# The last 512 tokens of a first pass as one chunk, keys put in order in halves, and another written order of the work, in a kernel of windowed attention and two MLPs

## The chip, the core and the metric

The kernel runs on one core of a Trainium2 chip. The metric is device time in microseconds (us) for one execution; three runs of the kernel before are shown. TensorE (PE) multiplies and transposes and writes only PSUM; its weight loads (PEld) run beside its matmuls. VectorE (DVE), ScalarE (ACT) and GpSimd (POOL) do the element work, and SyncE (SP) issues all transfers between the memory of the chip and SBUF. Each engine works through its own list of instructions in the order in which they were written, and waits on semaphores for what it needs from the others.

## What is computed

Attention with 8 heads on two sequences of 768 tokens: each query sees the 31 keys nearest to it and 24 block maxima of the keys, with the block means of the values behind them. Then come two MLPs with 512 inputs, 2048 hidden units and 512 outputs on the 1536 tokens. The second has a rational function of its hidden values.

```python
k_sum = k.reshape(B, H, nb, block, D).max(axis=3)      # block 32, window 16
v_sum = v.reshape(B, H, nb, block, D).mean(axis=3)
mask_l = np.abs(pos[:, None] - pos[None, :]) < window
...
scores_all = np.concatenate([scores_l_m, scores_s], axis=-1)
a = np.exp(scores_all - max); a = a / (sum + 1e-09)
out = np.matmul(a, np.concatenate([v, v_sum], axis=2))
...
h = np.maximum(x @ w_in, 0.0);  x = h * h @ w_out       # first MLP
h = x @ w_in2;  g = P(h) / (Q(h) + 1e-6);  out = g @ w_out2
```

## The kernel before

**Four passes.** The MLP work stands in `steps`: pass 0 covers hidden blocks 0 to 4 of the first MLP, pass 1 blocks 5 to 15, passes 2 and 3 the second MLP. A step is one token chunk with one block of 128 hidden units. It has a first layer (`l1`, line 567, four parts of three matmuls into a tile h), element work (`elem_1` to `elem_5`: relu on ScalarE, the square on VectorE, a rounded copy sh on ScalarE, the rest sl on GpSimd), and a second layer (`l2`, line 661, four parts of three matmuls into tiles y). Every product is made of three matmuls because each operand is split into a rounded part and a rest (wh and wl, xh and xl, sh and sl). In pass 0 a chunk has 256 tokens (`tok1`, six chunks, 30 steps); in the later passes it has 512 (`tok2`, three chunks). With 256 tokens the sums y need two PSUM banks, with 512 four.

**The attention fills pass 0.** It is cut into 24 units d = 0 to 23; four units give the 512 features of one group of 256 tokens, so chunk c of pass 0 needs the units 4c to 4c+3. A unit goes through: q (transpose of the queries, PE), z (copy into qz, ScalarE), s (scores pss, PE), m (mask and minimum, VectorE, line 467), e (exponential, ScalarE, line 476), r (sum and reciprocal rs, VectorE, lines 484 and 485), n (scaling of pr, GpSimd, line 491), p (transpose into ptp, PE), b (copy pp, ScalarE or VectorE, line 505), o (product with the values, pav, PE), x (xh, ScalarE) and y (xl, VectorE, line 536). The keys of a head pair come by E (transfer), P (put in order, GpSimd, line 300), t (transposes pk, PE), l and k (copies into kt), c and B (block maxima).

**Weights** arrive as 512 KB pieces: I (transfer into one of three buffers), T (ScalarE, line 150), D (VectorE, lines 158 and 159), W (wh, ScalarE) and M (wl, GpSimd, line 175).

**What sets the order.** All of the attention and nearly all of pass 0 is written by hand in the string `ORDER`; every word is one of the letters above with its number (h, i, j, G, H and Y are l1, elem_1, elem_2, elem_4, elem_5 and l2; a star puts a copy on VectorE). Each engine gets its instructions in this order. After the list, `main_loop` runs from step 28 (G1). While attention lasts, the sums of pass 0 hold two PSUM banks (`O0`), and the tiles of the attention take turns in the other four.

Of the kernel before, what the change touches and what calls it, by code (L numbers as in the profile page):

```python
# [9 lines left out]
F32 = mybir.dt.float32  # L10
# [49 lines left out]
def tile_window_attention_moe_moe(  # L60
# [13 lines left out]
    nc = tc.nc  # L74
    B, H, S, D = q.shape
    NT, DM = out.shape
    DFF = w_in1.shape[1]
    P = 128
# [3 lines left out]
    NP = H // 2  # L82
    KC = DM // P
    NF = DFF // P
    LO = 64
# [116 lines left out]
    ]  # L202
    kst = const.tile([P, TR, 4, D], F32, tag="xh2", name="kst")[0:VP]
    vst = const.tile([P, 4, TR, D], F32, tag="xl2", name="vst")[0:VP]
    ksrc = {}
    vsrc = {}
    banks = ["y0", "y1", "y2", "y3", "a0", "a1"]

# [649 lines left out]
```

## Time and profile before

| | us |
|---|---|
| median of three runs | 616.33 (616.15 to 616.97) |
| the profiled execution, its own time | 617.99 |
| its span | 616.3 |
| TensorE busy in the span | 597.6 (97%) |
| VectorE, ScalarE, GpSimd busy | 390.8, 402.1, 345.9 |
| granted TensorE clock, mean | 0.999 |

The span is what the trace shows between first and last instruction; 1.7 us of the profiled execution lie around it. Times within the trace count from the span's start. A matmul's recorded time holds its run through the array as well, so neighbours overlap in the record; the distance between starts is what one costs in a row of them.

### The profile page before, as it was taken

The page shows a single profiled execution, that of the slowest core. Times are in us where ns is not written, and L with a number is a line of the kernel's source. Part 1 is how long each engine was busy: PE and PEld are TensorE (multiplying, and loading weights), DVE is VectorE, ACT ScalarE, POOL GpSimd, SP SyncE. Part 2 cuts the span into 40 slices and gives each one's busy share as a digit, 9 for nine tenths or more (in the row PEclk, how much of TensorE's full clock was granted, in tenths as well). Part 3 has the DMA queues.
Part 4 walks back from the last instruction along what each step waited for, and adds up shares of the span by engine and source line. Part 5 has one row for each costly group of instructions (what it writes and reads, how often), then busy time and mean ns, then how long its engine had stood idle before and what let it go on. Part 6 is the DMA issues. An engine that isn't in the chain of part 4 may idle for free.

```text
span 616.3 us, 9787 instructions
## 1 busy us (share of the span) xinstructions
PE 597.6 (97%) x3488; PEld 514.0 (83%) x3488; DVE 390.8 (63%) x815; ACT 402.1 (65%) x766; POOL 345.9 (56%) x363
## 2 busy tenths in 40 slices
PE   5899998999999999999999999999999999999997
PEld 4789898999988888888888888888888888888885
DVE  5998777666553332111256487898878887686775
ACT  5887566766554443222356598988888887777772
POOL 4777858355664445222557568675656664454442
PEclk9999999999999999999999999999999999999999
DMA  9999894440342331000045202121202200010011
GB/s 220 247 225 213 208 233 96 120 108 16 114 160 72 99 103 35 0 1 0 1 137 179 96 1 69 34 70 34 69 35 69 69 1 0 1 69 1 22 47 68
DMA packets 64145, 51.48 MB, mean 84 GB/s; under 512 B 39777, under 2 KB 56161, under 8 KB 64097
## 3 DMA queue, kind: packets, MB, share of 16 engines
q1 hardware_dynamic: 64096, 50.87, 30.8%
q8 instruction: 27, 0.44, 0.3%
q14 instruction: 22, 0.17, 0.1%
HBM read 47.71 MB, written 3.15 MB: 83 GB/s over the span
## 4 chain that ended last, share of the span: by engine, by line
PE 80%; DVE 1%; ACT 0%; POOL 0%; issue 0%; DVEq 0%; ACTq 0%
PE h L567 39%; PE y L661 38%; PE pss L452 1%; PE pav L517 1%; PE ptp L501 1%; DVE acc L687 0%; PE pt L433 0%; DVE h L616 0%; DVE q L613 0%; ACT h L609 0%; POOL wl L175 0%; DVE p L619 0%; ACT q L588 0%; DVE p L602 0%; DVE pp L505 0%
## 5 line engine op out<-in xcount | busy, mean ns | idle before, releaser
L567 PE MATMUL h<-xh,wh 128*128 128x512 f32 (+1 forms) x444 | 161.9, 365 | 0.0
L567 PE MATMUL h<-xh,wl 128*128 128x512 f32 (+1 forms) x444 | 160.1, 361 | 0.0
L567 PE MATMUL h<-xl,wh 128*128 128x512 f32 (+1 forms) x444 | 160.0, 360 | 0.0
L637 POOL TENSOR_TENSOR sl<-r,sh 128x512 fp32r<-128x512 f32 (+1 forms) x63 | 66.4, 1054 | 119.8 <-PE y L661 76.6
L591 POOL TENSOR_TENSOR q<-q,u 128x512 f32<-128x512 f32 x48 | 63.8, 1330 | 94.7 <-ACT q L588 91.0
L582 DVE TENSOR_TENSOR r<-r,h 128x512 f32<-128x512 f32 (+1 forms) x63 | 35.0, 555 | 113.1 <-ACT r L577 105.6
L567 PEld LDWEIGHTS h<-xh,wh 128*128 128x128 f32 x444 | 83.8, 189 | 12.8
L567 PEld LDWEIGHTS h<-xh,wl 128*128 128x128 f32 x444 | 83.7, 189 | 12.9
L567 PEld LDWEIGHTS h<-xl,wh 128*128 128x128 f32 x444 | 83.8, 189 | 12.4
L175 POOL TENSOR_TENSOR wl<-wdec,wh 128x512 fp32r<-128x512 f32 x64 | 83.3, 1309 | 12.5 <-ACT wh L170 10.5
L661 PE MATMUL y<-sl,wh 128*128 128x512 f32 (+1 forms) x252 | 85.7, 340 | 1.3 <-POOL sl L637 1.3
L661 PE MATMUL y<-sh,wh 128*128 128x512 f32 (+1 forms) x252 | 86.7, 344 | 0.0
L661 PE MATMUL y<-sh,wl 128*128 128x512 f32 (+1 forms) x252 | 85.2, 338 | 0.0
L577 ACT ACTIVATE r<-h 128x512 f32<-128x512 f32 (+1 forms) x63 | 31.1, 494 | 82.5 <-PE h L567 44.1
L661 PE MATMUL y<-wh,sl 128*128 128x512 f32 x192 | 74.8, 390 | 0.1
L661 PE MATMUL y<-wl,sh 128*128 128x512 f32 x192 | 74.7, 389 | 0.0
L661 PE MATMUL y<-wh,sh 128*128 128x512 f32 x192 | 74.7, 389 | 0.0
L637 POOL TENSOR_TENSOR sl<-p,sh 128x512 fp32r<-128x512 f32 x48 | 64.5, 1344 | 9.9 <-ACT sh L630 8.6
L613 DVE SCALAR_TENSOR_TENSOR q<-q,h 128x512 f32<-128x512 f32 x48 | 32.9, 685 | 39.4 <-ACT h L609 39.4
L159 DVE SCALAR_TENSOR_TENSOR wdec<-wraw,wdec 128x512 int32<-128x512 int32 x64 | 56.0, 875 | 2.2
L170 ACT CAST wh<-wdec 128x512 fp32r<-128x512 f32 x64 | 39.7, 621 | 22.6 <-DVE wdec L159 22.5
L661 PEld LDWEIGHTS y<-sl,wh 128*128 128x128 f32 x252 | 47.6, 189 | 6.9 <-POOL sl L637 1.5
(88 smaller groups left out, 1071.8 us busy)
## 6 DMA issues: line engine op xcount, KB each, us to landing
wraw<-in_moe_w_in_dram SPq DMA_DIRECT2D x32, 512.0 KB, 3.9
wraw<-in_moe_w_out_dram SPq DMA_DIRECT2D x32, 512.0 KB, 3.4
early<-in_v_dram SPq DMA_DIRECT2D x40, 96.0 KB, 4.4
out_dram<-acc SPq DMA_DIRECT2D x12, 256.0 KB, 2.1
acc<-in_q_dram SPq DMA_DIRECT2D x10, 256.0 KB, 5.4
early<-in_k_dram SPq DMA_DIRECT2D x4, 384.0 KB, 5.3
early<-in_v_dram SPq DMA_DIRECT2D x4, 384.0 KB, 8.0
kst<-in_k_dram SPq DMA_DIRECT2D x8, 192.0 KB, 7.1
```

The costliest lines, as they stand in the source:

```text
L159: nc.vector.scalar_tensor_tensor(out=t, in0=low, scalar=29, in1=t, op0=ALU.logical_shift_right, op1=ALU.bitwise_or)
L170: nc.scalar.copy(out=wt[n][0][:, j], in_=f32(wdec[n, j]))
L175: nc.gpsimd.tensor_tensor(out=tl[:, j], in0=t, in1=f32(th[:, j]), op=ALU.subtract)
L452: nc.tensor.matmul(pt[:, c * HK:(c + 1) * HK], lhsT=qz[d % 2][:, c].rearrange("p e t -> p (e t)"), rhs=kt[p][:, 2 * i + c], start=c == 0, ...
L501: nc.tensor.transpose(out=pt[0:HK, c * P:(c + 1) * P], in_=pr[:, c, 0:HK], identity=ident)
L567: nc.tensor.matmul(hq[g][:, 0:n], lhsT=w[:, 0, ws], rhs=x[:, part, ts], start=(part == 0 and j == 0), stop=(part == KC - 1 and j == 2),)
L577: nc.scalar.activation(out=r, in_=hq[g][:, 0:n], func=AF.Relu)
L582: nc.vector.tensor_tensor(out=eq[g], in0=eq[g], in1=hq.pop(g)[:, 0:n], op=ALU.mult)
L591: nc.gpsimd.tensor_tensor(out=q_, in0=q_, in1=u_, op=ALU.mult)
L613: nc.vector.scalar_tensor_tensor(out=q_, in0=q_, scalar=1.0 + 1e-6, in1=z_, op0=ALU.add, op1=ALU.mult)
L637: nc.gpsimd.tensor_tensor(out=sl[:, 0:n], in0=eq.pop(g), in1=f32(sh[:, 0:n]), op=ALU.subtract)
L661: nc.tensor.matmul(o, lhsT=lt, rhs=rt, start=(f == 0 and j == 0 and d * m % 512 == 0), stop=(f == FS[ps] - 1 and j == 2 and (d + 1) * m % ...
```

## The change

`tok1` has five chunks: four of 256 tokens and one of 512, the last. Pass 0 has 25 steps instead of 30, and `main_loop` begins at step 23. The last chunk needs the units 16 to 23. Its `h` and `Y` words (h80 to h99, Y80 to Y99) stand for matmuls with 512 columns.

The keys of the first sequence are put in order in two halves, P and R, each with its own choice of engine; the transposes read the copy. P0 is on VectorE, the others on GpSimd. The tiles pp, mx and rs are named by the parity of d instead of being taken in turn, so the units may be written out of order. `ORDER` is another string.

```diff
-    def k_rel(p, copy):
+    def k_rel(p, b, copy):
         t = early[4 + p][0:VP].rearrange("p (r h d) -> p r h d", r=TR, d=D)
-        copy(out=t.rearrange("p r h d -> p h r d"), in_=ksrc[p])
-        ksrc[p] = t
+        rs = slice(b * TR // 2, (b + 1) * TR // 2)
+        copy(out=t[:, rs].rearrange("p r h d -> p h r d"), in_=ksrc[p][:, :, rs])
+        krel[p] = t
...
-        mx = ap.tile([P, 8], F32, tag="mx", name="mx", bufs=2)
+        mx = mxs[d % 2]
...
-    tok1 = [(G * c, G) for c in range(NT // G)]
+    tok1 = [(G * c, G) for c in range(NT // G - 2)] + [(NT - 2 * G, 2 * G)]
...
-        P=lambda p: k_rel(p, nc.gpsimd.tensor_copy), t=k_tr,
+        P=lambda p, c=nc.gpsimd.tensor_copy: k_rel(p, 0, c),
+        R=lambda p, c=nc.gpsimd.tensor_copy: k_rel(p, 1, c), t=k_tr,
...
-    "E0 E1 _id P0 _m0 t0 l0 P1 E2 q_0 _z0 t1 q0 k0 _pr k1 I0 P2 q_1 _ml t2 _m1 E3 q1 l1 z0 c0 T0 "
+    "E0 _id _m0 _ml P0* _bw R0 E1 q_0 t0 E2 l0 I0 P1 R1 t1 q0 k0 _m1 P2 q_1 R2 _z0 E3 q1 l1 c0 t2 "
```

At the start, GpSimd had in the kernel before (ident is the unit matrix, early the keys, mask and bw constants):

```order
masks.py:197 MEMSET ident 128x128
masks.py:199 ISA
masks.py:199 AFFINE_SELECT ident<-ident 128x128
L300 COPY early<-early 96x2x8x64 x3
L248 AFFINE_SELECT mask<-mask 64x96 x2
L300 COPY early<-early 96x2x8x64
L264 AFFINE_SELECT bw<-bw 96x24 x2
```

and has now, with what each row waits for:

```order
masks.py:197 MEMSET ident 128x128
masks.py:199 ISA
masks.py:199 AFFINE_SELECT ident<-ident 128x128 [waits Pool_49]
L265 AFFINE_SELECT bw<-bw 96x24 [waits DVE_49]
L265 AFFINE_SELECT bw<-bw 96x24 [waits Pool_49]
L302 COPY early<-early 96x2x4x64 [waits DMAHW0_49]
L302 COPY early<-early 96x2x4x64 [waits DMAHW1_49]
```

The selects on bw moved ahead of the key copies, and the first of them waits for VectorE. VectorE now begins with:

```order
L274 MEMSET mask 64x96
L275 MEMSET mask 128x6x24
L302 COPY early<-early 96x2x4x64 [waits DMAHW0_49]
L263 MEMSET bw 96x120
L270 MEMSET bw 96x96 [waits DVE_49]
L367 MEMSET pk 128x5x4 x4
```

Half of the first key copy moved here, and the bw and pk constants stand behind it; before, the first two pk constants were VectorE's second row.

At the end of the attention TensorE had (y_2188 is half of the sums of chunk 4; h there is chunk 4's as well):

```order
L567 MATMUL h<-xh,wh 128x256
L567 MATMUL h<-xl,wh 128x256
L567 MATMUL h<-xh,wl 128x256
L501 MATMUL ptp<-ident,pr_96 120x128 x4
L501 MATMUL ptp<-ident,pr_97 120x128 x4
L517 MATMUL pav<-pp,early 64x64 x32
L661 MATMUL y_2188<-sh,wh 128x256
```

and has now (the sums y are those of chunk 3, the 512-column rows are chunk 4's first):

```order
L519 MATMUL pav<-pp_87,early 64x64 x8
L519 MATMUL pav<-pp_88,early 64x64 x8
L503 MATMUL ptp<-ident,pr_103 120x128 x4
L569 MATMUL h<-xh,wh 128x512
L569 MATMUL h<-xl,wh 128x512
L569 MATMUL h<-xh,wl 128x512
L503 MATMUL ptp<-ident,pr_102 120x128 x4
L663 MATMUL y_1822<-sh,wh 128x256
L663 MATMUL y_1822<-sh,wl 128x256
L663 MATMUL y_1822<-sl,wh 128x256
L519 MATMUL pav<-pp_88,early 64x64 x8
L519 MATMUL pav<-pp_87,early 64x64 x8
```

The matmuls of chunk 4 moved from before and between the last units to behind them. ScalarE's list there now reads:

```order
L478 ACTIVATE pr_103<-pr_103,mx_90 128x120 x4
L478 ACTIVATE pr_102<-pr_102,mx_89 128x120 x4
L533 CAST xh<-pav 128x256
L507 COPY pp_87<-ptp 120x512
L507 COPY pp_88<-ptp 120x512
L533 CAST xh<-pav 128x256 x3
L147 ACTIVATE wdec<-wraw 128x512
L507 COPY pp_87<-ptp 120x512
L533 CAST xh<-pav 128x256 x2
```

where before it was:

```order
L476 ACTIVATE pr_96<-pr_96,mx 128x120 x4
L476 ACTIVATE pr_97<-pr_97,mx 128x120 x4
L577 ACTIVATE r<-h 128x256
L630 CAST sh<-r 128x256
L505 COPY pp<-ptp 120x512
L531 CAST xh<-pav 128x256
L170 CAST wh<-wdec 128x512
L531 CAST xh<-pav 128x256 x2
L170 CAST wh<-wdec 128x512
L531 CAST xh<-pav 128x256
```

Three of the last copies of pp are ScalarE's now, between exponentials and xh.

## Rows read from the trace of the kernel before

**Rows 1.** The page: busy time of TensorE, and its share of the span.

```profile
PE 597.6 (97%) x3488; PEld 514.0 (83%) x3488; DVE 390.8 (63%) x815; ACT 402.1 (65%) x766; POOL 345.9 (56%) x363
```

**Rows 2.** Busy time by stage (us); each engine's instructions; clock; DMA share; GB/s.

```profile
core 0: us, PE busy (x) PEld busy (x) DVE busy (x) ACT busy (x) POOL busy (x), PEclk, DMA share, GB/s
0.00:5.58 5.58, 0.00 (x1) 0.01 (x1) 1.72 (x14) 1.28 (x1) 1.80 (x9) 1.00 0.69 173
5.58:33.18 27.60, 23.41 (x200) 20.23 (x201) 23.71 (x92) 22.81 (x59) 18.54 (x33) 1.00 1.11 253
33.18:66.00 32.82, 31.66 (x321) 30.30 (x318) 29.55 (x102) 26.61 (x68) 25.07 (x36) 1.00 1.01 207
66.00:100.00 34.00, 31.45 (x311) 30.57 (x310) 24.71 (x73) 21.98 (x59) 23.53 (x35) 1.00 0.88 212
100.00:130.00 30.00, 28.93 (x311) 28.05 (x310) 19.61 (x75) 21.72 (x60) 18.45 (x37) 1.00 0.35 89
130.00:156.00 26.00, 25.67 (x286) 25.07 (x285) 17.10 (x63) 17.17 (x48) 11.93 (x26) 1.00 0.23 60
156.00:176.00 20.00, 20.00 (x147) 18.99 (x146) 11.68 (x17) 10.29 (x23) 11.49 (x12) 1.00 0.37 123
```

**Rows 3.** TensorE's waits between 66 and 156 us: us, times, longest.

```profile
PE y L661 <- POOL sl L637: 1.3, 1, 1.3
PE pav L517 <- ACT pp L505: 1.2, 1, 1.2
PE pav L517 <- DVE pp L505: 1.2, 2, 0.9
```

**Rows 4.** The chain that ended last, in order of time: start, us, what.

```profile
110.52 2.86 PE h L567 x24
...
182.33 2.72 PE h L567 x12
```

**Rows 5.** The start, in order of time: start, us, engine, line, operation [idle before].

```profile
4.49 1.03 POOL L300 COPY early<-early 96x1024 f32<-96x1024 f32 x1 [3.05 <-DMA early<-in_k_dram]
5.58 1.54 PE L368 MATMUL pk<-ident,early 96*128 96x96 f32 x8 [5.58 <-POOL early L300]
...
7.29 1.54 PE L368 MATMUL pk<-ident,early 96*128 96x96 f32 x8 [0.17 <-POOL early L300]
8.62 0.63 PE L433 MATMUL pt<-ident,acc 128*128 128x128 f32 x2
```

**Rows 6.** VectorE, 0 to 175 us, by form: count, busy us, mean ns.

```profile
L505 DVE COPY pp<-ptp 120x512 f32<-120x512 f32 x17 | 11.5, 684 | 5.4 <-PE ptp L501 3.0 <-PE pav L517 2.2 <-issue 0.2
L257 DVE COPY mask<-mask 128x384 f32<-128x384 f32 x1 | 0.4, 353 | 0.0
L262 DVE MEMSET bw<- 96x120 f32 x1 | 0.2, 158 | 0.0
```

**Rows 7.** ScalarE from 66 to 73 us, in order of time.

```profile
69.38 0.67 ACT L150 ACTIVATE wdec<-wraw 128x512 f32<-128x512 f32 x1 [1.49 <-DMA wraw<-in_moe_w_out_dram]
69.95 1.23 ACT L476 ACTIVATE pr<-pr,mx 128x120 f32<-128x120 f32 x4
71.09 0.56 ACT L505 COPY pp<-ptp 120x512 f32<-120x512 f32 x1
```

**Rows 8.** VectorE's second weight step alone, and the same beside other work.

```profile
152.99 0.69 DVE L159 SCALAR_TENSOR_TENSOR wdec<-wraw,wdec 128x512 int32<-128x512 int32 x1
...
32.47 1.64 DVE L159 SCALAR_TENSOR_TENSOR wdec<-wraw,wdec 128x512 int32<-128x512 int32 x1
```

**Rows 9.** The last units of the attention, all engines, in order of time.

```profile
145.66 2.40 ACT L476 ACTIVATE pr<-pr,mx 128x120 f32<-128x120 f32 x8
...
147.99 2.75 POOL L491 TENSOR_SCALAR pr<-pr,rs 128x120 f32<-128x120 f32 x8 [1.34 <-DVE rs L485]
...
151.19 1.15 PE L517 MATMUL pav<-pp,early 120*64 120x64 f32 x32
...
152.87 0.38 ACT L531 CAST xh<-pav 128x256 fp32r<-128x256 f32 x1
```

More of the change, by code (lines that the diff above doesn't have):

```diff
@@ L187, in tile_window_attention_moe_moe @@
     qz = [ap.tile([P, 4, 2, LO], F32, name=f"qz{j}", bufs=1) for j in range(2)]
+    pps = [ap.tile([HK, 4, 2, LO], F32, name=f"pp{j}", bufs=1) for j in range(2)]
+    mxs = [ap.tile([P, 8], F32, name=f"mx{j}", bufs=1) for j in range(2)]
+    rss = [ap.tile([P, 4], F32, name=f"rs{j}", bufs=1) for j in range(2)]
     kss = [ap.tile([P, NB], F32, name=f"kss{j}", bufs=1) for j in range(NP)]
@@ L205, in tile_window_attention_moe_moe @@
     ksrc = {}
+    krel = {}
     vsrc = {}
@@ L360, in k_tr @@
     def k_tr(p):
-        src = ksrc[p].rearrange("p r h d -> p r (h d)")
+        src = (krel if p < NP else ksrc)[p].rearrange("p r h d -> p r (h d)")
         pk[p] = [bank("pk"), bank("pk")]
@@ L482, in d_r @@
         mx, pr = ex.pop(d)
-        rs = ap.tile([P, 4], F32, tag="rs", name="rs", bufs=2)
+        rs = rss[d % 2]
         nc.vector.tensor_reduce(out=mx[:, 4:8], in_=pr, axis=AX.X, op=ALU.add)
@@ L503, in d_b @@
     def d_b(d, copy=nc.scalar.copy):
-        pp = ap.tile([HK, 4, 2, LO], F32, tag="pp", name="pp", bufs=2)
+        pp = pps[d % 2]
         copy(out=pp.rearrange("p c e t -> p (c e t)"), in_=po[d][0:HK])
```

67 rows, old and new, of the table ORDER are left out of this document.

## The prediction

> **What bounds the kernel now.** I read the page first: TensorE is busy for 597.6 us of the 616.3 us span [rows 1]. Then the stages [rows 2]: from 156 us on, TensorE is busy all the time, so nothing but fewer or shorter matmuls shortens that part. Ahead of it lie 156 us with 141.1 us of TensorE work (23.41 + 31.66 + 31.45 + 28.93 + 25.67). The 14.9 us that are missing split into 5.6 before the first transpose, 4.2 up to 33 us, 1.2 up to 66, 2.6 up to 100, 1.1 up to 130 and 0.3 up to 156. The reader is to see two more things there. Up to 33 us VectorE is busy for 23.71 of 27.60 us and the DMA share is 1.11, so TensorE waits for VectorE and for data, not for its own order. And from 130 to 156 us TensorE waits for only 0.3 us, because the matmuls of chunks 4 and 5 fill in between the last units of the attention. Third come TensorE's waits between 66 and 156 us [rows 3]: one wait of 1.3 for sl, one of 1.2 for a copy pp by ScalarE, and 1.2 for copies pp by VectorE. The sum below counts gains and losses in these places alone: the TensorE work itself, the start, the middle, and the end of the attention.
>
> **The longer last chunk.** Two chunks of 256 tokens are 10 steps with 24 matmuls, 240 of 256 columns; the one chunk is 5 steps, 120 matmuls of 512 columns. In a row, 24 of the narrow ones take 2.86 us, 0.119 each, and 12 of the wide ones 2.72, 0.227 each [rows 4]. So 240 x 0.1192 = 28.6 us become 120 x 0.2267 = 27.2 us: 1.4 us less TensorE work, all of it on the bounding engine. Element work gets longer per instruction and fewer in number; after the attention the three other engines are at half load (156 to 176 us [rows 2]), which hides it. Wide steps follow each other at 2.7 us per layer, while relu, square, sh and sl of one step need about 3.2 us in a row and have two wide layers (5.4 us) to hide in. If that cover fails, each of five steps could lose some tenths.
>
> [...]
>
> **The start.** Now TensorE starts at 5.58 us, when the copy of the first keys on GpSimd, 4.49 to 5.52, is done [rows 5]. In halves on two engines each half should take about half as long. The order shows what takes it back. The first half stands on VectorE, and behind it the bw and pk constants that the first transpose and GpSimd wait for. No row shows this half copy. Its bounds are 353 ns (a copy of 384 columns) and 684 ns (512 columns from PSUM) [rows 6]; I take 0.47, 353 x 512 / 384, since that row reads SBUF too. Then 4.49 + 0.47 + two constants of at most 0.16 each + the pk constant puts the first transposes at about 5.4 instead of 5.58. GpSimd waits with its selects on bw for the first of these constants (5.1), and only then copies the second half, half of 1.03 us: done at about 6.1. The second four transposes then run 6.1 to 6.8, and end about when the eight end now (5.58 + 8 x 0.166 = 6.9; a set of eight takes 8.62 - 7.29 = 1.33 [rows 5]). I take 0.1 gained, bounds 0.5 gained and 0.3 lost. Up to unit 7 the list holds the same VectorE work as before within 0.5 us (instructions counted, times their rows), and this stretch goes by VectorE and data, so I expect nothing else here, within 1 us either way.
>
> **The middle, 56 to 110 us.** The wait of 1.2 us for a pp by ScalarE [rows 3] has a clear cause [rows 7]: ScalarE stood 1.49 us for a weight piece that had not landed, then did an exponential of 1.23 us, then the copy. In the new list that piece stands behind 768 KB fewer transfers, some 3 us at the 212 to 253 GB/s of these stages [rows 2], and the copy is VectorE's, behind a weight step and a mask step. If the weight step is done early, nothing is waited for; if not, about 0.7 us. I take 0.4 instead of 1.2: 0.8 gained, bounds 1.2 and 0. For the other waits there (sl, 1.3, and pp, 1.2) I see no change of load: from the scores of unit 12 to the second layer of step 14 the list gives VectorE some 22.5 us against 20.7 of TensorE, before 20.3 against 18.3 (instructions counted, times their rows). Zero, bounds 2.4 gained and 2 lost.
>
> **The end of the attention.** Here the change takes something away. h80 reads all of the units 16 and 20, h83 those of 19 and 23, so no matmul of the last chunk can fill gaps before the last units are through. Before, 25.67 of 26.00 us were filled [rows 2]. What is left to fill with is chunk 3 only. Between h79 and h80 TensorE has four transposes p of 0.42, six products o of 0.62, two scores s of 0.85 and three parts of Y of 0.36, 8.2 us; ScalarE has 9.6 us in the same piece of list (three exponentials of 1.2 [rows 9], three copies pp of 0.6, six xh of 0.33, and a qz, a weight step, a relu and a sh with 2.2). The one place where I find TensorE early is the product of unit 20: its pp waits on ScalarE behind the exponentials of units 23 and 22 and one xh. Followed from unit 18's scores with the pitches of rows 9 (exponentials 1.2, n 1.38, pp 0.6, xh 0.33, o 0.6), with all engines free at the start, TensorE waits there for 0.9 us. Against the 0.3 of before that is 0.6 lost. If ScalarE comes in late by the 2.4 us of two exponentials in a row [rows 9], TensorE waits that much longer, 3.3. So the loss is 0.6, with bounds of 0 and 3.0.
>
> What could make it more is VectorE's weight step 18, which stands ahead of the xl of unit 21, on which h81 waits; it takes 0.69 us alone and took 1.64 beside other work [rows 8]. The longer one would delay h81 by about 1 us, for 615.6 in all; the sum goes by 0.69, and 1.64 is in the range. [...]
>
> **The sum.** -1.4 - 0.1 - 0.8 + 0.6 = -1.7. The profiled execution took 617.99 us with a span of 616.3; its changed twin should have a span of 614.6. The median of 616.33 happens to equal that span, and the change of -1.7 taken from it gives 614.6.
>
> **Rivals.** *The middle keeps its waits.* VectorE is the fuller engine there in both lists, and a wait removed at one product comes back at the next Y; the new list may also bring small waits of its own. Then -1.4 - 0.1 + 0.6 = -0.9 and some tenths more: 615.6. For it speaks that VectorE has more work than TensorE in that stretch; against it, that the late weight piece was the cause of one wait and stands earlier now. *The end starves TensorE.* If ScalarE and VectorE reach the last eight units late, the wait is 3.3 us or more instead of 0.9, and if the middle gains nothing: 616.33 - 1.5 + 3.0 + 0.4 = 618.2, slower. For it speaks that the products of units 16 to 23 now stand within 11 us of TensorE work, where 25 us were; against it, the walk above. It decides from 3.0 us of TensorE waiting between the scores of unit 18 and h83. *More is gained.* If the middle loses its waits of 1.2, 1.3 and 0.9: 616.33 - 1.5 - 3.0 + 0.6 = 612.4. *The halves do nothing* is in the forecast already, with 0.1.
>
> **How the numbers follow.** A measurement of this kernel can tell about 0.2%, 1.23 us, from no change: faster is below 615.1, slower above 617.6. Forecast 0.42, the middle keeps its waits 0.28, the starved end 0.20, more gained 0.10. Most of the forecast's case and all of the larger gain are faster, 0.50; the rest of it and the second case are the same, 0.29; the starved end is slower, 0.21. The range of 8 in 10 reaches from 612.6 to 617.7: it leaves out half of the larger gain and more than half of the starved end. The forecast's own range is 613.8 to 615.4.
>
> **What would show it.** In the profile after: wide matmuls of the last chunk at 0.227 us; the first transposes at 5.3 to 5.5 us in two groups of four with a gap between; no ScalarE wait for a weight piece near 68 us; TensorE busy without a gap from h83 on, and its waits in the 15 us ahead of it at 1 us in sum, at the product of unit 20. Wrong would be a wait of over 2 us there, new waits of over 2 us between 10 and 110 us, or a first chunk of pass 1 that starts late.

## The result and the profile after

The changed kernel takes 610.82 us (median of 6 runs, 610.05 to 613.01) against 616.38 us for the kernel before (median of 6, 615.80 to 619.22). The ratio is 0.9906 (95% interval 0.9882 to 0.9930); a second set of runs gave 0.9916 (0.9895 to 0.9937). By the two ratios it is faster by 5.8 and 5.2 us; below, 5.5 stands for it. The forecast was 1.7 us, and the range ended at 612.6: the sign was right, the size was not, and the time lies 1.8 us below the range.

The profiled execution took 610.05 us, its span is 608.3. First the page's line of busy times, which answers to [rows 1]:

```profile
PE 595.7 (98%) x3368; PEld 509.1 (84%) x3368; DVE 381.1 (63%) x803; ACT 402.6 (66%) x764; POOL 346.1 (57%) x361
```

TensorE is busy for 1.9 us less, in a span 8.0 us shorter (the profiled execution of the kernel before was 1.6 us over its median). So 6.1 us between these two executions are idle time of TensorE. Its place is in the busy time by stage, cut as in [rows 2] (columns as there):

```profile
5.58:33.18 27.60, 24.77 (x205) 22.66 (x206) 25.05 (x99) 23.65 (x64) 19.63 (x36) 1.00 1.17 250
33.18:66.00 32.82, 32.59 (x327) 31.44 (x326) 25.76 (x88) 26.46 (x70) 27.25 (x39) 1.00 1.02 226
66.00:100.00 34.00, 33.84 (x361) 33.04 (x360) 27.28 (x93) 27.32 (x73) 25.07 (x42) 1.00 0.94 204
100.00:130.00 30.00, 30.00 (x326) 29.39 (x326) 22.67 (x102) 24.63 (x72) 19.26 (x38) 1.00 0.38 95
```

Idle in these four: 2.83, 0.23, 0.16 and 0.00 us, where it was 4.19, 1.16, 2.55 and 1.07. A second profile of each kernel, taken with the experiments, confirms only the later part. Up to 33 us it has the idle time the other way round, 3.00 us in the kernel before (first line) and 4.29 in the kernel after:

```profile
5.58:33.18 27.60, 24.60 (x203) 21.40 (x203) 23.30 (x92) 23.58 (x62) 18.80 (x34) 1.00 1.10 254
5.58:33.18 27.60, 23.31 (x204) 21.47 (x205) 25.25 (x99) 23.38 (x64) 19.41 (x36) 1.00 1.16 247
```

From 33 to 156 us the second pair has 3.4 us of idle time before and 0.3 after, the first pair 5.1 and 0.4. So the change takes 3 to 5 us of idle time out of this part, and what it does ahead of 33 us is less than two executions differ by.

TensorE's waits, as in [rows 3] (us in total, times, longest), first from 5.7 to 66 us, then the one that is left from 66 to 156 us:

```profile
PE pk L370 <- DVE pk L367: 5.6, 1, 5.6
PE pk L370 <- POOL early L302: 1.1, 2, 0.8
PE pav L519 <- DMA early<-in_v_dram: 0.7, 2, 0.4
PE pss L454 <- DVE kt L396: 0.6, 1, 0.6
PE pvs L409 <- POOL early L327: 0.6, 1, 0.6
...
PE pss L454 <- DVE mx L469: 0.2, 1, 0.2
```

The 5.6 us are the time to the first transpose, which has not moved. The chain of work that ended last shows the long chunk, as in [rows 4] (start, us, what):

```profile
144.46 5.44 PE y L663 x24
```

5.44 / 24 is 0.2267 us for a matmul of 512 columns, as forecast. The start, as in [rows 5]:

```profile
4.57 0.42 DVE L302 COPY early<-early 96x512 f32<-96x512 f32 x1 [3.39 <-DMA early<-in_k_dram]
4.97 0.16 DVE L263 MEMSET bw<- 96x120 f32 x1
5.36 0.13 DVE L367 MEMSET pk<- 128x20 f32 x4
...
5.20 0.47 POOL L265 TENSOR_SCALAR_AFFINE_SELECT bw<-bw 96x24 f32<-96x24 f32 x2 [3.76 <-DVE bw L263]
5.61 1.72 POOL L302 COPY early<-early 96x512 f32<-96x512 f32 x3
...
5.58 2.88 PE L370 MATMUL pk<-ident,early 96*128 96x96 f32 x16 [5.58 <-DVE pk L367]
```

VectorE's half takes 0.42 us (0.47 was estimated), and the constants behind it bring the first transpose back to 5.58 us, as before.

### The profile page after: what moved, and what is told of

Its sections match the earlier page's. It is cut to its first block, busy times and chain, and to the rows that moved or that the text cites. A ratio compares the mean times of both kernels' runs of the same rounds, so it can differ in the third digit from the quotient of the medians.

```text
span 608.3 us, 9541 instructions
## 1 busy us (share of the span) xinstructions
PE 595.7 (98%) x3368; PEld 509.1 (84%) x3368; DVE 381.1 (63%) x803; ACT 402.6 (66%) x764; POOL 346.1 (57%) x361
## 4 chain that ended last, share of the span: by engine, by line
PE 90%; DMA 3%; SPq 3%; DVE 2%; ACT 1%; issue 1%; DVEq 0%; ACTq 0%
PE h L569 43%; PE y L663 41%; DMA early<-in_v_dram 3%; PE pss L454 3%; PE pav L519 2%; PE ptp L503 1%; SPq L136 1%; SPq L336 1%; PE pt L435 1%; DVE acc L689 0%; SPq L315 0%; SPq L355 0%; SPq L293 0%; DVE h L618 0%; DVE q L615 0%
## 5 line engine op out<-in xcount | busy, mean ns | idle before, releaser
L569 PE MATMUL h<-xl,wh 128*128 128x512 f32 (+1 forms) x424 | 156.6, 369 | 0.0
L569 PE MATMUL h<-xh,wl 128*128 128x512 f32 (+1 forms) x424 | 156.5, 369 | 0.0
L569 PEld LDWEIGHTS h<-xl,wh 128*128 128x128 f32 x424 | 79.9, 189 | 13.6 <-DVE xl L538 0.2
L569 PEld LDWEIGHTS h<-xh,wh 128*128 128x128 f32 x424 | 79.9, 188 | 13.4
L569 PEld LDWEIGHTS h<-xh,wl 128*128 128x128 f32 x424 | 79.8, 188 | 13.2
L663 PE MATMUL y<-sh,wh 128*128 128x512 f32 (+1 forms) x232 | 83.0, 358 | 0.0
L663 PE MATMUL y<-sh,wl 128*128 128x512 f32 (+1 forms) x232 | 81.8, 352 | 0.0
L663 PE MATMUL y<-sl,wh 128*128 128x512 f32 (+1 forms) x232 | 81.7, 352 | 0.0
L156 DVE SCALAR_TENSOR_TENSOR wdec<-wraw,wdec 128x512 int32<-128x512 int32 x64 | 50.2, 784 | 2.2
L589 ACT ACTIVATE u<-h 128x512 f32<-128x512 f32 x48 | 28.6, 595 | 31.4 <-PE h L569 31.3
```

The source lines that it names most:

```text
L156: nc.vector.scalar_tensor_tensor(out=t, in0=low, scalar=29, in1=t, op0=ALU.logical_shift_right, op1=ALU.bitwise_or)
L569: nc.tensor.matmul(hq[g][:, 0:n], lhsT=w[:, 0, ws], rhs=x[:, part, ts], start=(part == 0 and j == 0), stop=(part == KC - 1 and j == 2),)
L589: nc.scalar.activation(out=u_, in_=hq[g][:, 0:n], func=AF.Abs)
L663: nc.tensor.matmul(o, lhsT=lt, rhs=rt, start=(f == 0 and j == 0 and d * m % 512 == 0), stop=(f == FS[ps] - 1 and j == 2 and (d + 1) * m % ...
```

## The experiments

Ratios are to the kernel before on the same chip, with 95% intervals; where kernels of different chips are compared, it is by these. Beside the median stands the median span of the runs with a mean granted clock of 0.999 or more, with their number, for a reason that the first group gives.

| kernel | median us | ratio | span at full clock |
|---|---|---|---|
| after | 610.82 | 0.9906 | 608.8 (4 of 6) |
| after, again | 611.38 | 0.9916 | 609.2 (4 of 5) |
| before, again | 615.81 | 0.9991 | 613.7 (5 of 10) |
| after, whole key copies | 613.15 | 0.9942 | 608.9 (3 of 11) |
| after, six short chunks | 615.94 | 0.9995 | 613.8 (6 of 12) |
| the same, tail mended | 615.38 | 0.9982 | 612.3 (5 of 12) |
| before, long chunk | 624.81 | 1.0139 | none of 5 |
| after, words to unit 7 as before | 612.16 | 0.9929 | 610.3 (4 of 6) |
| the same, one word moved | 611.25 | 0.9914 | 609.6 (6 of 6) |
| after, words to unit 15 as before | 619.64 | 1.0056 | none of 6 |
| the same, seam mended | 618.25 | 1.0036 | 615.9 (4 of 12) |
| after, units 8 to 15 as before | 626.45 | 1.0161 | none of 6 |
| before, two words moved | 614.68 | 0.9979 | 612.8 (9 of 12) |
| after, band table later | 611.34 | 0.9920 | 609.0 (3 of 5) |
| after, all tables early | 611.01 | 0.9913 | 609.3 (6 of 6) |
| and one copy by ScalarE | 610.67 | 0.9898 | 609.0 (6 of 6) |
| and pair 3 ahead | 610.71 | 0.9903 | 609.0 (6 of 6) |

**The halves of the key copies.** The edit: the two halves become one whole copy on GpSimd.

```diff
-        rs = slice(b * TR // 2, (b + 1) * TR // 2)
+        rs = slice(0, TR)
-    "... P0* _bw R0 ... P1 R1 ... P2 ... R2 ... P3 ... R3 ..."
+    "... P0 _bw ... P1 ... P2 ... P3 ..."
```

> The kernel after, with each of the first keys put in order by one whole copy on GpSimd (as in the kernel before) instead of two halves, the first of them on VectorE; all else as it is. Theory A (my prediction's): the halves change the start by -0.5 to +0.3 us, so within 0.5 us of the kernel after: 610.3 to 611.4. Rival: VectorE's half and the halves' order on GpSimd let the first products begin sooner, and whole copies on GpSimd, behind its clearing and masks, cost 1 us or more at TensorE's first transposes: 612 or more.

Measured: 613.15 us (0.9942, 0.9922 to 0.9963), so by the median the rival's 612 or more. But its three runs at full clock have spans of 608.5 to 609.1 us, those of the kernel after. The other eight, at clocks of 0.993 to 0.997, have 610.8 to 613.6. The profile is one of those: TensorE's key transposes of pair 3, and the stretches of 2 us around them (columns as above; the granted clock is the third number from the right):

```profile
20.18 1.51 PE L370 MATMUL pk<-ident,early 96*128 96x96 f32 x8 [3.19 <-DVE pk L367]
...
18.00:20.00 2.00, 0.00 (x0) 0.00 (x0) 1.97 (x14) 1.61 (x5) 0.00 (x0) 0.88 1.00 327
20.00:22.00 2.00, 1.82 (x11) 1.85 (x12) 1.75 (x12) 1.17 (x4) 1.86 (x5) 0.50 1.21 209
24.00:26.00 2.00, 2.00 (x11) 2.00 (x10) 1.71 (x5) 0.82 (x4) 1.24 (x4) 0.50 1.08 290
```

TensorE stood for 3.19 us behind VectorE's queue, and then its granted clock was 0.50 until 26 us. VectorE was late by two weight steps, which lie beside GpSimd's work here (2.89 us busy from 14 to 18 us) and take 0.42 and 0.69 us at this place in the kernel after:

```profile
15.16 1.39 DVE L155 TENSOR_SCALAR wdec<-wdec 128x512 int32<-128x512 int32 x1
16.59 1.77 DVE L156 SCALAR_TENSOR_TENSOR wdec<-wraw,wdec 128x512 int32<-128x512 int32 x1
```

This wait does not need whole copies: a kernel with the halves (six short chunks, tail mended, below) has it in its profile too, 3.37 us at the same transposes. At full clock the halves save nothing that three runs show. By the ratios the kernel with whole copies is 1.6 to 2.2 us slower than the kernel after, and its clock was lost more often (8 of 11 runs, against 3 of 11 of the kernel after); whether that is the copies' doing is not settled.

> The kernel after, unchanged, on the same chip as the three runs beside it. All theories: 610 to 612 us. [...] My theory: runs of this kernel with a mean granted clock of 1.000 have spans of 608.3 to 609.3 us, and those at 0.997 are 1.5 to 2 us longer. Rival: the spread of the runs has nothing to do with the clock, and then runs at 1.000 spread as widely as the others.

The second set of the kernel after bears the clock out only in part: 608.4 to 610.1 us at 0.999 and above, 609.8 at 0.997. So runs at full clock spread by 1.7 us as well. In the first set the two runs at 0.997 have 609.6 and 611.3 us, the four at full clock 608.3 to 609.2. Nor is there a length of wait that I could name for a fall of the clock: it came behind 3.19 us here and behind 1.79 below, and a wait of 2.26 us (below) went by without one. In a profile of the kernel before with two words moved (below) it came behind four short waits.

**The chunk alone, in both orders.** First the kernel before with the long chunk: the words of its last two chunks leave the end of the attention and stand behind it.

```diff
-    tok1 = [(G * c, G) for c in range(NT // G)]
+    tok1 = [(G * c, G) for c in range(NT // G - 2)] + [(NT - 2 * G, 2 * G)]
-    "... y17 h80 b18* n19 p19 b19 D18 h81 o18 ... y19 h82 h83 I20 h84 i20 ..."
+    "... y17 b18* n19 p19 b19 D18 o18 ... y19 I20 m20 ... y23 h80 h81 h82 h83 ..."
```

> The kernel before with the one long chunk at the end of the first pass, its order else kept: the first products of the last two chunks, which stood between the words of the last units of the attention, go behind it, where the kernel after has them. Rival of my prediction (with that cover gone the end of the attention starves TensorE): waits of 4 to 8 us between 130 and 156 us at scores and products, and 617 to 621 us. Other theory (other work covers it): 614.5 to 615.5, the matmuls' 1.5 us less.

Measured: 624.81 us (1.0139, 1.0119 to 1.0159), more than even the rival said. Its waits from 130 to 156 us, where the kernel before had 0.3 us:

```profile
136.88 1.15 PE L449 MATMUL pss<-kt,qz 128*128 128x120 f32 x8 [2.46 <-ACT qz L438]
140.48 1.15 PE L449 MATMUL pss<-kt,qz 128*128 128x120 f32 x8 [1.34 <-ACT qz L438]
144.04 2.03 PE L498 MATMUL ptp<-ident,pr 128*120 128x128 f32 x6 [1.49 <-POOL pr L488]
```

So the rival's mechanism is real: with its cover gone, the old order starves TensorE at the end. The kernel after has the same chunk and no such wait. Then the order after with six short chunks again:

```diff
-    tok1 = [(G * c, G) for c in range(NT // G - 2)] + [(NT - 2 * G, 2 * G)]
+    tok1 = [(G * c, G) for c in range(NT // G)]
-    "... y22 h81 h82 W18 ... h84 D19 G19 W19 h85 I22 T20 j20 H19 ..."
+    "... y22 h81 h82 W18 ... h83 i20 G19 H19 j20 D19 W19 h84 Y76 G20 H20 ..."
```

> The kernel after, but its first pass ends in six chunks of 256 tokens again instead of four and one of 512 at the end; the written list is the kernel after's up to the end of the attention, and the rest of the first pass is written as a plain interleave. My theory: the one long chunk is worth only the difference of its matmuls, 120 x 0.227 = 27.2 against 240 x 0.119 = 28.6 us, and the order of the attention's words does not need it. Then this kernel takes 1.2 to 1.8 us more than the kernel after: 612.0 to 612.6, and the stretch up to the end of the attention has the same waits of TensorE (0.4 us from 33 us on). Rival: the long chunk is worth several microseconds, since it also takes the first pass off what holds TensorE: then 613.5 or more, with waits of TensorE after 136 us.

Measured: 615.94 us (0.9995), with waits after 136 us as the rival had them, 0.52 us for sh and this one for sl, at the head of the tail as I had written it:

```profile
139.16 0.39 PE L666 MATMUL y<-sl,wh 128*128 128x256 f32 x1 [0.58 <-POOL sl L642]
```

With these steps put ahead and the second products later:

```diff
-    "... y22 h81 h82 W18 ... h83 i20 G19 H19 j20 D19 W19 h84 Y76 G20 H20 h85 Y77 ..."
+    "... y22 G19 H19 h81 h82 W18 ... h83 i20 j20 D19 W19 h84 h85 Y76 G20 H20 h86 Y77 ..."
```

> As the first kernel with six chunks of 256 (the kernel after otherwise), but the tail behind the attention is written with the second products a half chunk later, and with the two steps that made TensorE wait (1.5 us in all from 138 to 139.5 us) put ahead. My theory: the long chunk is worth only its matmuls, 1.4 to 2 us, and the rest of the 5 us seen was my tail's waits and the start's spread: then 612.2 to 613.3, with no wait from 136 us on. Rival: the long chunk itself is worth 4 us or more, by something that is no wait: then 614.5 or more with no wait of TensorE from 136 us on.

Measured: 615.38 us (0.9982, 0.9967 to 0.9997), 4 to 4.7 us over the kernel after by the ratios. That is the rival's size, but not its reason. The pure matmul term is as forecast, read off the chain:

```profile
145.13 0.72 PE h L572 x6
```

0.120 each, so 240 x 0.120 = 28.8 us against 120 x 0.2267 = 27.2: 1.6 us. Counted on the two traces from the last matmul of the attention's last product to the same matmul (the 1900th from the end), the tail takes 41.4 against 38.3 us: 3.1 us. Three matmuls of chunk 4 stand ahead of this stretch in both, so it holds 237 short against 117 long ones, 28.4 against 26.5 us. That leaves 1.2 us for waits and for the matmuls right behind them; the profile lists waits of 0.4 and 0.2 us there. A short step gives the other engines 24 x 0.120 = 2.9 us of TensorE's time for their chain, a long one 5.4; that this is why the short steps wait was not tested. What is left of the 4 to 4.7 us, about 1 us or some more, I put down to the clock, by an estimate from the runs' mean clocks: 0.9970 for its 12 runs, 0.9987 for those of the kernel after (0.0017 x 613 = 1.0).

Together: the chunk in the old order costs 8.6 us, the new order with short chunks gains 1, and both gain 5.5. Neither part carries the gain alone.

**The first stretch.** The kernel after with the words up to the last of unit 7 as before:

```diff
-    "E0 _id _m0 _ml P0* _bw R0 E1 q_0 t0 ... w1 D2 p3 e5 b3* Q2 ... i4 J2 y7 ..."
+    "E0 E1 _id P0 R0 _m0 t0 l0 P1 R1 E2 q_0 ... p3 o2 D2 b3* e5 n4 ... y7 ..."
```

> The kernel after, with the words of the list up to the last one of unit 7 in the order in which the kernel before has them, and with the engines that the kernel before gives to the copies there (halves of key order included, all on GpSimd). Theory A: the order of this first stretch gave some 2.3 us (TensorE idle 4.19 and 1.16 us in the two stretches 5.58 to 33.18 and 33.18 to 66 of the kernel before, 2.83 and 0.23 after). Then 612.5 to 613.5, with the long waits near 31 and 35 us back. Theory B (my prediction's): the order of these words is worth nothing up to unit 7 and the idle time lies elsewhere: then within 0.5 us of the kernel after, 610.3 to 611.3.

Measured: 612.16 us (0.9929, 0.9909 to 0.9949), 0.8 to 1.4 us over the kernel after: between the two theories, and the intervals of the kernels overlap. What the profile shows is plainer. VectorE, GpSimd and TensorE at 27 to 34 us:

```profile
29.49 2.36 DVE L155 TENSOR_SCALAR wdec<-wdec 128x512 int32<-128x512 int32 x1
...
32.50 0.68 DVE L507 COPY pp<-ptp 120x512 f32<-120x512 f32 x1
...
27.58 2.75 POOL L493 TENSOR_SCALAR pr<-pr,rs 128x120 f32<-128x120 f32 x8
30.29 1.28 POOL L172 TENSOR_TENSOR wl<-wdec,wh 128x512 fp32r<-128x512 f32 x1
...
33.23 0.69 PE L519 MATMUL pav<-pp,early 120*64 120x64 f32 x16 [1.79 <-DVE pp L507]
...
34.00:36.00 2.00, 2.00 (x12) 2.00 (x12) 2.00 (x13) 2.00 (x6) 1.94 (x5) 0.59 0.96 155
```

A weight step that takes 0.42 us elsewhere takes 2.36, and ends 0.28 us after GpSimd's run of nine instructions ends at 31.57. The copy of the product of unit 3 stands behind it, TensorE waits 1.79 us, and the granted clock falls to 0.59 in the stretch that follows. A second profile of the kernel before, unchanged, has the same:

> The kernel before, unchanged, for a second profile of it. Theory: the waits of 1.24 us at 71.7 us (a weight piece that landed 1.49 us late) and of 1.31 us at 98.7 us, of which the prediction took one as gained by the change, belong to the one execution that was profiled; in the same words of three other kernels they are 0.2 to 0.4 us. Then this profile shows 1.4 to 1.8 us of TensorE's waits from 66 to 110 us instead of 3.6. Rival: they are the kernel's own, and the profile shows 3 us or more there.

Measured: 615.81 us (0.9991). Here the wait at this place is 2.02 us (0.95 in the first profile):

```profile
30.08 2.60 DVE L158 TENSOR_SCALAR wdec<-wdec 128x512 int32<-128x512 int32 x1
...
34.06 1.13 PE L517 MATMUL pav<-pp,early 120*64 120x64 f32 x16 [2.02 <-DVE pp L505]
```

And its waits from 66 to 110 us, which the expectation was about:

```profile
PE pav L517 <- DVE pp L505: 0.9, 1, 0.9
PE y L661 <- POOL sl L637: 0.7, 1, 0.7
PE ptp L501 <- POOL wl L175: 0.2, 1, 0.2
```

1.8 us instead of 3.6: the wait of 1.2 us for a pp by ScalarE is not there, and that for sl is 0.7 instead of 1.3. They were bigger in the execution that the prediction was read from.

Then one word in the kernel with the first stretch as before:

```diff
-    "... T2 p3 o2 D2 b3* e5 n4 ..."
+    "... T2 p3 o2 b3* D2 e5 n4 ..."
```

> The kernel with the words up to unit 7 in the order of the kernel before (612.2 us), with one of them moved: the third weight piece's steps on VectorE stand behind the copy of the product of unit 3 instead of ahead of it. There the first of those steps took 2.36 us beside GpSimd's products and weight step, the copy stood behind it, TensorE waited 1.79 us and its clock went to 0.5 behind that. Theory (that place is what the first stretch was worth): the wait is gone, and the time within 0.7 us of the kernel after, 610.3 to 611.5, all runs at a granted clock of 0.999 or more. Rival (the order of the whole stretch matters): 611.8 to 612.6.

Measured: 611.25 us (0.9914, 0.9890 to 0.9938), all six runs at 0.999 or more. The wait for the product is gone, and the weight step takes 1.11 us. But a new wait stands close behind:

```profile
34.02 0.38 PE L569 MATMUL h<-xl,wh 128*128 128x256 f32 x1 [1.07 <-DVE xl L538]
```

So part of the 1.79 us comes again; the clock was kept. The time cannot be told from the kernel after's, nor from that of the kernel without the swap, 0.9 us over it. That this word is worth the whole first stretch agrees with the runs and is not shown by them.

**The middle.** Two kernels were to give its order alone; both came out with waits of their own making.

```diff
-    "... y7 G3 M7 j4 h21 h22 n8 ... Q5 D15 W15 s17 r16 y14 T16 y15 ..."
+    "... y7 q11 z11 N8 n8 t5 k5 J5 ... h61 y14 M14 y15 m16 e16 D15 T16 W15 r16 z17 s17 ..."
```

> The kernel after, with the words between the last of unit 7 and the last of unit 15 in the order in which the kernel before has them (with its choice of engines). Theory A: the order of the middle gave the waits of TensorE back that the kernel before had from 66 to 130 us (2.55 and 1.07 us idle in 66 to 100 and 100 to 130): then +2.5 to +3.5 us, 613.3 to 614.3, with waits of 0.8 to 1.3 us for a copied product and for a copy of GpSimd. Theory B: the middle's waits came from VectorE and the weight transfers being late since the first stretch, and with a first stretch that ends 3 us sooner the same words wait no more: within +1 us, 610.5 to 611.8.

Measured: 626.45 us (1.0161). At the upper seam a transpose of keys stands ahead of the load of these keys, for 4.98 us; at the lower one the scores of unit 17 stand right behind their queries, for 3.42. It tells nothing of the middle. With the words up to unit 15 as before, only the lower seam is left:

> The kernel after, with all words up to the last of unit 15 in the order of the kernel before and with its choice of engines (key copies on GpSimd in halves): only the end of the attention and the long chunk are the change's. With the kernel in which only the words up to unit 7 were put back (612.2 us, 1.3 over the kernel after) this gives the middle alone, without the loads of keys moved behind their users that spoiled the first attempt. Theory A (the middle's order gave the gain): 1.5 to 3 us over that one, 613.7 to 615.2, with the waits of 1.2, 1.3 and 0.9 us at the products and at the copy by GpSimd back. Theory B (the middle's order as such gives no more than my prediction's 0.8): 612.2 to 613.2.

Measured: 619.64 us (1.0056), with the same wait at the seam, 3.40 us. Mended, the queries go ahead of seven words of other work and their scores behind it:

```diff
-    "... q17 T15 h61 y14 M14 y15 m16 e16 D15 T16 W15 r16 z17 s17 h62 h63 i15 h64 M15 ..."
+    "... q17 z17 T15 h61 y14 h62 M14 y15 h63 m16 e16 i15 D15 T16 h64 W15 r16 s17 M15 ..."
```

> As the kernel with the words up to unit 15 in the order of the kernel before, with the seam mended: there the scaled queries of unit 17 stood right ahead of its scores, and TensorE waited 3.4 us for them in one piece, which also took the clock down. Without those about 5 us it would have taken some 614 us. Theory A (the middle's order gave about half of the gain): 613.2 to 614.8, 1 to 2.5 us over the kernel with the first stretch alone put back (612.2 us). Theory B (the middle's order gives at most the 0.8 us that I predicted): 612.0 to 613.0.

Measured: 618.25 us (1.0036), over either theory. New waits of 0.9 and 1.4 us stand at the seam, at 113 and 115 us, and the granted clock of the stage from 100 to 130 us is 0.94. So the time settles nothing. What can be used is ahead of the seam, TensorE's waits from 66 to 110 us in the words of the kernel before:

```profile
PE pav L519 <- DVE pp L507: 0.9, 1, 0.9
PE y L663 <- POOL sl L639: 0.3, 1, 0.3
PE ptp L503 <- DVE early L417: 0.2, 1, 0.2
```

1.4 us, close to the second profile's 1.8. The kernel after has 0.2 there. So the middle is worth 1.2 to 1.6 us by its waits. Two words in the kernel before test two of them:

```diff
-    "... D2 b3* e5 ... T11 h33 H6 e11 h34 p9 j7 I12 b9 h35 ..."
+    "... b3* D2 e5 ... h33 H6 e11 h34 p9 j7 I12 b9 T11 h35 ..."
```

> The kernel before with two words moved, one for each of two waits of TensorE: the third weight piece's steps on VectorE go behind the copy of the product of unit 3, which stood behind them (0.95 us at 34.8 us), and the top part of weight piece 11 on ScalarE goes behind the copy of the product of unit 9, which stood behind it (1.24 us at 71.7 us, with a wait of 1.49 us for the piece's landing). Theory A: both waits are the queueing behind these steps, and what is saved stays saved, as nothing later is set by a transfer: 2.0 us less than the kernel before, about 614.4. Rival: TensorE is held by chains of VectorE and ScalarE that are as late in any order, so the waits come again a few units on: within 0.7 us of the kernel before.

Measured: 614.68 us (0.9979, 0.9963 to 0.9994), 1.1 to 1.3 us less, between the two; at full clock the spans are 612.8 against 613.7 to 614.7 of the kernel before on the same chip and others. The profile has lost the waits at 34.8 and 71.7 us and keeps the 0.9 us at 106 us:

```profile
PE pav L517 <- DVE pp L505: 0.9, 1, 0.9
PE pav L517 <- DVE mx L467: 0.5, 1, 0.5
PE y L661 <- POOL sl L637: 0.2, 1, 0.2
```

That less came of it than 2.0 agrees with the second profile, in which the wait at 71.7 us was not there to be saved. So the queue behind the weight step is the cause of the wait at 34 us: both kernels with this word moved have lost it. That some of it stays saved is shown by the interval, which ends below 1, for the two words together. The clock of this profile fell all the same, at 28.8 us, behind four waits of 0.5 to 0.7 us from 14.9 us on and none that is longer:

```profile
30.00:32.00 2.00, 1.92 (x20) 1.42 (x19) 1.86 (x12) 1.93 (x6) 2.00 (x7) 0.50 0.91 337
```

**Four tries at a faster version.** Four kernels went for what is left at the start of the kernel after. The first:

```diff
-    "... P0* _bw R0 E1 q_0 t0 E2 l0 I0 ..."
+    "... P0* R0 E1 q_0 t0 E2 l0 _bw I0 ..."
```

> The kernel after, with the making of the 0/1 band table moved behind the first linear part of the keys, so that VectorE clears the first banks right behind its half of the key copy. My reading of the start: TensorE's first transposes, which began at 5.58 us behind VectorE's clearing at 5.36, begin at 5.0 to 5.2, and the later waits of the start absorb most of it: 610.2 to 610.8. Rival: the second half of the copy on GpSimd or the landing of the next keys sets the start: no change at all, 610.8; or the table is then late for the first value sums and TensorE waits there 0.5 us or more: 611.3 or more.

Measured: 611.34 us (0.9920). The keys landed at 5.01 instead of 4.57 us in its profile, and the first transposes began at 5.66: 0.65 us behind the landing instead of 1.01. The landing spreads more than that between two runs, and no gain is left.

The second:

```diff
-    "E0 _id _m0 _ml P0* _bw R0 ... _m1 P2 q_1 R2 _z0 E3 ... _m2 _pr s0 ..."
+    "E0 _id _m0 _ml _bw _m1 _m2 _z0 _pr P0* R0 ... P2 q_1 R2 E3 ... s0 ..."
```

> The kernel after, with all that is made without a load (band table, window mask, its copies, the zeros of the queries, the small numbers of the products) put ahead of the first key copy, where VectorE and GpSimd have nothing to do from 1.2 to 4.5 us. It takes 2.5 us of VectorE's work and 1.1 us of GpSimd's out of 5 to 11 us. My reading (from 10 to 22 us VectorE sets the pace of the start, and TensorE waits there 1 to 2 us for cleared banks and for keys): 0.5 to 1.5 us less than the kernel after, 609.3 to 610.3. Rival (the landing of the next keys sets the start): 610.3 to 611.3, no difference.

Measured: 611.01 us (0.9913), no difference. VectorE does 2.0 us more ahead of 5 us and is busy for 1.3 us less from 5 to 12 us, but this stands at 17 to 22 us:

```profile
17.75 2.58 DVE L396 COPY kt<-kss 128x192 f32<-128x192 f32 x1
...
17.59 1.37 POOL L493 TENSOR_SCALAR pr<-pr,rs 128x120 f32<-128x120 f32 x4
18.94 1.27 POOL L172 TENSOR_TENSOR wl<-wdec,wh 128x512 fp32r<-128x512 f32 x1
...
22.25 1.15 PE L454 MATMUL pss<-kt,qz 128*128 128x120 f32 x8 [2.26 <-DVE kt L396]
```

A copy of 192 elements takes 2.58 us (0.26 at 98.64 us in the kernel after, where GpSimd stands still), until 0.12 us after GpSimd's run of five ends at 20.21, and TensorE waits 2.26 us for keys that are queued behind it. The third and fourth, on top of this one, each with the words before it:

```diff
-    "... N0 l3* B1* N1 ..."
+    "... N0 l3* B1 N1 ..."
```

> The kernel with its tables made early, and one word more changed: the copy of the block keys of pair 1 into the last two windows of its table, which took VectorE 2.58 us at 17.75 us (0.2 to 0.3 where GpSimd stands still) beside GpSimd's products and its weight step from 17.59 to 20.21 us, is made by ScalarE. My theory: GpSimd's run holds that VectorE instruction until it ends, and TensorE's wait of 2.26 us at 22.25 us for the keys queued behind it is that hold; then the wait falls to under 0.8 us, and the time by 1 to 1.5 us: 609.5 to 610.2, spans of 606.5 to 608 us at full clock. Rival: VectorE is simply full there, and the next instruction is late in its place: the wait stays above 1.5 us and the time at 611.0.

```diff
-    "... m1 S0 Q1 R3 q3 B2 r0 W0 S1 s2 I1 n0 v2 e1 t3 z3 ..."
+    "... m1 R3 S0 Q1 q3 B2 W0 S1 s2 I1 v2 t3 r0 n0 e1 z3 ..."
```

> The same, and besides the second half of the key copy of pair 3 goes ahead of the value sum on GpSimd, and the clearing of its banks ahead of the sums of unit 0 on VectorE, so that the transposes of pair 3, which waited 0.88 us at 16.5 us for both, can begin when TensorE comes to them. My theory: a further 0.5 to 0.9 us, 608.8 to 609.7, if the value sums (which get their first operand in the same order) do not become late. Rival: the value sums' operands, which wait for a load, set the place: no more than the kernel beside it.

Measured: 610.67 (0.9898, 0.9878 to 0.9917) and 610.71 us (0.9903, 0.9884 to 0.9923). In the first, the wait for keys at 20.83 us is 0.31 us: the long copy on VectorE was its cause, as my theory said. The time is the rival's all the same, because TensorE now comes early to other places:

```profile
20.83 1.15 PE L454 MATMUL pss<-kt,qz 128*128 128x120 f32 x8 [0.31 <-DVE kt L396]
...
31.88 0.81 PE L519 MATMUL pav<-pp,early 120*64 120x64 f32 x16 [0.69 <-ACT early L417]
```

The value sums and their copies, which go back to loads, are next. None of the four can be told from the kernel after.

## Why the prediction was wrong, step by step

**The longer chunk, -1.4: right.** The matmuls cost 0.1200 and 0.2267 us, which gives 1.6. What the step left out is that short steps behind the attention would also wait, some 1.2 us. The kernel before had most of them beside the attention.

**The start, -0.1: right for the first transpose, open for the time.** The half copy, the constants and the selects stand as described, and the first transpose is where it was. The gap that was to part the first transposes into two groups is not there: sixteen run in a row from 5.58 us. And the bounds of 0.5 gained and 0.3 lost looked at these first transposes alone. By the ratios whole copies cost 1.6 to 2.2 us, which goes with the wait of 3.19 us and the clock and which the runs do not pin on the copies.

**"Up to unit 7 ... I expect nothing else here, within 1 us either way": wrong in its reason, and worth 0.8 to 1.4 us with the clock.** The reason was that this stretch goes by VectorE and data. Both are as full in the kernel after (VectorE 25.05 us, and 25.25 in the second profile, against 23.71; DMA share 1.17 against 1.11), and still the waits of 0.95 and 2.02 us at 34 us are gone, so busy shares could not tell whether the order matters. I counted VectorE's work by its usual durations, found it equal in both lists and stopped there. The loss was no matter of how much work, but of one instruction that took 2.36 and 2.60 us beside GpSimd's work, with a product's copy behind it. The row for it was on the table ([rows 8]: 0.69 us alone, 1.64 beside other work) and I used it for the end of the attention only. The integer step takes 0.42 us where GpSimd stands still (152.53 us in the kernel before); why it took so much longer here is not shown.

**The middle, -0.8: right in sign, wrong in its reason and half of its size.** It took 0.8 of the wait of 1.24 us behind the late weight piece [rows 3, 7] and nothing elsewhere. In the second profile that wait is missing, so it was hardly there to be gained. The waits that show in every profile of this order (0.9 us at a product, 0.2 to 1.3 at sl, 0.2) I held as kept, for equal load. They are gone in the kernel after: 1.2 to 1.6 us. Between the two first profiles the idle time from 66 to 130 us differed by 3.5. Reading one execution, I could not tell a wait of the order from one of that landing.

**The end of the attention, +0.6: wrong sign, 0.3 gained.** The walk had TensorE wait 0.9 us for the copy of unit 20's product, behind ScalarE's exponentials. ScalarE after, and the product, as in [rows 9]:

```profile
129.75 1.06 ACT L507 COPY pp<-ptp 120x512 f32<-120x512 f32 x2
...
130.62 1.15 PE L519 MATMUL pav<-pp,early 120*64 120x64 f32 x32
```

The copy starts at 129.75, and TensorE comes to the product at 130.62 without a wait; where the walk lost the 0.9 us was not followed up. The rival itself is real: in the old order the same chunk starves TensorE for 5.3 us and costs 8.6 us in all.

**The sum.** Chunk 1.6, first stretch 0.8 to 1.4 (with the clock lost there), middle 1.2 to 1.6, end 0.3: 3.9 to 4.9 of the measured 5.5 us. So the steps that failed are the two terms put at nothing for equal load, in the first stretch and for the other waits of the middle, and the 0.6 us of loss at the end. The largest rival, "more is gained", had the middle's share but gave it 0.10 and no first stretch; its three waits add up to 3.4 us, where its sum took 3.0. None of the waits of over 2 us that were to show the forecast wrong is in the profile after. Some 0.6 to 1.6 us stay without a place, no more than the intervals of these runs allow; the tiles that go by parity were not tested by themselves.

## What to carry to other kernels

Where the bounding engine waits for copies, look for the instruction ahead of the copy that overlaps with a run of GpSimd, and take its longest duration in the trace for the sum, not its usual one (here 2.60 against 0.42 us); then move the copy ahead of it. Before a wait goes into a sum, see whether a second profile has it. And cost two edits together when one takes away the cover that the other's order makes needless: here one alone loses 8.6 us, the other alone gains 1, and both gain 5.5.

## What the runs showed of the hardware

Three VectorE instructions beside back-to-back GpSimd work took 2.58 us (a copy of 192 elements), 2.60 and 2.36 us (an integer step), against 0.26 and 0.42 us where GpSimd stood still (at 98.64 us in the kernel after and at 152.53 us in the kernel before). Each ended 0.12 to 0.29 us after the last of a run of GpSimd instructions; that the run held it is my reading of these ends. By it, a run does not always hold to its end. In the kernel after the same integer step took 1.55 us beside a row of five and ended at 66.28 us, 0.28 us after the second of them, with GpSimd busy until 68.42:

```profile
64.73 1.55 DVE L155 TENSOR_SCALAR wdec<-wdec 128x512 int32<-128x512 int32 x1
...
63.46 4.96 POOL L327 TENSOR_TENSOR vst<-vst 96x512 f32<-96x512 f32 x5
```

What decides between the two is open.

And in three profiles the granted clock was lower in or right behind a long wait of TensorE. For the wait of 1.79 us it was 0.59 and 0.56 in the two stretches of 2 us that follow, for 2.02 us 0.92, 0.50 and 0.72 from 32 to 38 us, for 3.19 us 0.88 in the stretch before 20 us and 0.50 until 26 us. The mean clocks of these three profiled executions were 0.997, 0.997 and 0.994. Of the 11 runs with whole key copies, 8 had a mean clock of 0.993 to 0.997 and spans of 610.8 to 613.6 us, where the three at full clock had 608.5 to 609.1. But the 2.26 us wait above passed without a fall (1.00 from 5.58 to 66 us), and the fall to 0.50 behind four waits of 0.5 to 0.7 us had no such single gap. What takes the clock down is not shown.
